# Attention softmax: one VectorE operation on two columns for a tile's threshold and the older tile's guarded sum

## The chip, the core and the metric

The kernel runs on one core of one Trainium2 chip. The core has a matrix engine (TensorE, PE in the profile, with its weight loads as PEld), a vector engine (VectorE, DVE), a scalar engine (ScalarE, ACT), GpSimd (POOL) and a queue that issues DMAs (SP). Each engine works through its own instruction queue in order; a wait at the head of a queue holds everything behind it. The metric is the device time of one execution in microseconds; the time of a kernel is the median of its runs.

## The reference

Attention over 2 batches, 8 heads, 576 rows and head dimension 64, then two mixture-of-experts layers on the 1152 rows of 512 columns. Only the attention is touched:

```python
def _attn_ref(q, k, v, tau):
    scores = scale * np.matmul(q, k.transpose(0, 1, 3, 2))
    thresh = np.max(scores, axis=-1, keepdims=True) - tau
    scores = np.where(scores >= thresh, scores, -1000000000.0)
    scores = scores - np.max(scores, axis=-1, keepdims=True)
    attn = np.exp(scores)
    attn = attn / (np.sum(attn, axis=-1, keepdims=True) + 1e-09)
    return np.matmul(attn, v)
```

Of each row the scores below the maximum minus tau are dropped, the rest goes through exp, and the row is divided by its sum plus 1e-9.

## The kernel before

The attention is cut into 72 units of 128 rows by 576 scores (`at.units`). They go through a software pipeline written out by hand: `step` runs once for each t, and in one step different units stand at different stages. Unit t+2 gets its scores on PE (`scores`), unit t+1 (called `a`) its row maximum and its exp (`top`, `line`, `exp`), unit t (called `d`) its mask with the row sum, its guarded sum, its reciprocal and its scaling (`mask`, `guard`, `norm`), unit t-2 (called `x`) is transposed on PE (`turn`) and split into a high and a low part (`hi` on ACT, `lo` on DVE), and units t-3 to t-5 are multiplied with V (`mix`, `out`). Nothing reorders this: the order of the calls in `step` is the order in each engine's queue.

On DVE one step is, for the two units together: the mask of `d` (L306, tile `ex`, which multiplies the exp by the comparison with the threshold and leaves the row sum in column 3 of `d`'s statistics tile `st`; reading the accumulator is a row of its own), the row maximum of `a` (L287, a reduction over 576 scores in PSUM), `guard` (L310, `d`'s sum plus 1e-9), `line` (L292, `a`'s threshold from its negated maximum and `on`, which holds tau), and the reciprocal of `d`'s guarded sum (L314). Behind these come `lo` (L341, L344, tiles `etl` and `eth`), `xf` (L388) and the low part of a hidden tile (L492, tile `hl`). The four units of the first head pair take their threshold with two operations (L294, L295) since their scores are not prescaled.

ACT reads column 0 of `a`'s statistics in its exp (L302; L300 in the first head pair). The mask waits for that exp. POOL scales `d`'s tile by the reciprocal (L316); PE transposes it two steps later (L324).

Into the free time of PE the steps put matrix products of the first two experts (`fill`, `expert_fill`: L483 and L511 on PE, L489 on ACT, L492 on DVE). What of these is left when the attention ends (at about 255 us) runs behind it, and the experts' layers follow to the end. All statistics of a unit lie in one `st` tile of 8 columns, of which 6 buffers rotate.

Of the kernel before, what the change touches and what calls it, by code (L numbers as in the profile page):

```python
# [9 lines left out]
F32 = mybir.dt.float32  # L10
F32R = mybir.dt.float32r
AF = mybir.ActivationFunctionType
ALU = mybir.AluOpType
# [6 lines left out]
P = 128  # L20
# [3 lines left out]
HS = S // 2  # L24
# [5 lines left out]
def attention_two_moe_kernel(ctx, tc, qP, kP, qT, kT, vp, tau, wg, w1, w1s, w2, w2s, dp, m2w1s, m2w2, m2w2s, out):  # L30
    nc = tc.nc
    V, A, G, T = nc.vector, nc.scalar, nc.gpsimd, nc.tensor
# [4 lines left out]
    def pool(stack, name, bufs=1, **kw):  # L37
        return stack.enter_context(tc.tile_pool(name=name, bufs=bufs, **kw))

    cp = pool(ctx, "const")  # L40
# [7 lines left out]
    ones = cp.tile([P, P], F32, name="ones")  # L48
# [5 lines left out]
    tau_sb = cp.tile([P, 1], F32, name="tau_sb")  # L54
    warm = cp.tile([P, 1], F32, name="warm")
    A.activation(warm, ones[:, 0:1], AF.Exp)
    esc = cp.tile([P, 1], F32, name="esc")
    lin = cp.tile([P, 2], F32, name="lin")
    on = cp.tile([P, 1], F32, name="on")
    wg_sb = cp.tile([P, KT, E1], F32, name="wg_sb")  # L60
    wg2 = cp.tile([P, KT, 2 * E1], F32R, name="wg2")
    dp_sb = cp.tile([P, NT, E2], F32, name="dp_sb")
# [7 lines left out]
    def gap(p, n):  # L70
        gaps.append(n)
        p.tile([P, n // 4], F32, name=f"gap{len(gaps)}")

    gap(cp, 224)
    xh = cp.tile([P, KT, N], F32R, name="xh")
    xl = cp.tile([P, KT, N], F32R, name="xl")

# [44 lines left out]
    class Attention:  # L122
# [159 lines left out]
                    T.matmul(sc[:m, hf, :HS], lhsT=q, rhs=kk[:, hf * HS:(hf + 1) * HS],  # L282
                             start=i == 0, stop=i == len(ops) - 1)

        def top(self, u):
            st = u["st"] = self.pl.tile([P, 8], F32, tag="st", name="st", bufs=6)
            V.tensor_reduce(st[:, 0:1], u["sc"][:, :, :HS], axis=AX.XY, op=ALU.max, negate=not u["q"][0][0]["ws"])  # L287

        def line(self, u):
            st = u["st"]  # L290
            if not u["q"][0][0]["ws"]:
                V.tensor_scalar(st[:, 2:3], st[:, 0:1], -1.0, on, op0=ALU.mult, op1=ALU.subtract)  # L292
                return
            V.tensor_scalar(st[:, 1:2], st[:, 0:1], lin[:, 0:1], None, op0=ALU.mult)  # L294
            V.tensor_scalar(st[:, 2:3], st[:, 0:1], lin[:, 1:2], None, op0=ALU.subtract)  # L295

        def exp(self, u):
            ex = u["ex"] = self.pl.tile([P, 2, HS], F32, tag="ex", name="ex", bufs=4)
            if u["q"][0][0]["ws"]:
                A.activation(ex, u["sc"][:, :, :HS], AF.Exp, bias=u["st"][:, 1:2], scale=esc)  # L300
            else:
                A.activation(ex, u["sc"][:, :, :HS], AF.Exp, bias=u["st"][:, 0:1])  # L302

        def mask(self, u):
            st, ex = u["st"], u["ex"]
            V.scalar_tensor_tensor(ex, u["sc"][:, :, :HS], st[:, 2:3], ex, op0=ALU.is_ge, op1=ALU.mult,  # L306
                                   accum_out=st[:, 3:4])

        def guard(self, u):
            V.tensor_scalar(u["st"][:, 4:5], u["st"][:, 3:4], 1e-9, None, op0=ALU.add)  # L310

        def norm(self, u):
            st = u["st"]
            V.reciprocal(st[:, 5:6], st[:, 4:5])  # L314
            exf = u["exf"] = u["ex"].rearrange("p a b -> p (a b)")
            G.tensor_scalar(exf, exf, st[:, 5:6], 1.0, op0=ALU.mult, op1=ALU.mult)  # L316

        def turn(self, u):
            eg, exf = u["eg"], u["exf"]
# [87 lines left out]
        def step(self, fill, side):  # L407

            us, t = self.units, self.t
            un = lambda i: us[i] if 0 <= i < len(us) else None  # L410
            self.load()
            nxt, a, d, x, c, z, y = (un(t + i) for i in (2, 1, 0, -2, -3, -4, -5))
            if x:
                self.turn(x)
            if d:
                self.mask(d)
            if a:
                self.top(a)
            if d:
                self.guard(d)  # L420
            if a:
                self.line(a)
            if d:
                self.norm(d)
            for part, u in ((2, y), (1, z), (0, c)):
                for g in u["mix"] if u else ():
                    if g["head"]["exact"]:
                        self.mix(g, part)
            if x:
                self.hi(x)  # L430
            for u, late in ((z, False), (y, True)):
                for g in u["mix"] if u else ():
                    if late == (g["head"]["exact"] and g["head"]["h"] < H - 1):
                        self.out(g)
            if a:
                self.exp(a)
            fill(0, bool(c and c["mix"]))
            if x:
                self.lo(x)
            if nxt:  # L440
                self.scores(nxt)
            self.run(self.later)
            for g in c["mix"] if c else ():
                if not g["head"]["exact"]:
                    self.mix(g, 0)
            fill(1, bool(c and c["mix"] or z and z["mix"]))
            self.run(self.late)
            for w in self.work.pop(t, ()):
                w()
            side()  # L450
            self.t += 1
            return self.t < len(us) + 5
# [85 lines left out]
    with ExitStack() as att:  # L538
        ap = pool(att, "attn", side="right")
        ps_s = pool(att, "ps_s", 2, space=PSUM)  # L540
        ps_t = pool(att, "ps_t", 1, space=PSUM)
        ps_r = pool(att, "ps_r", 1, space=PSUM)
        banks.pool = ps = pool(att, "ps_m", 2, space=PSUM)
        at = Attention(ap, ps_s, ps_t, ps_r, ps)
        for p in range(H // 2):
            at.add_pair(0, p, 0, 256, True, p == 0)
        nA0 = len(at.units)
        for p in range(H // 2):
            at.add_pair(0, p, 256, 320, False)
        nA1 = len(at.units)  # L550
        for p in range(H // 2):
            at.add_pair(1, p, 0, S, False)
        at.plan()
        room = [2 * FT]
        at.load()
        V.tensor_scalar(on, tau_sb, 0.0, None, op0=ALU.is_ge)
        V.tensor_scalar(esc, on, 0.125, None, op0=ALU.mult)
        V.tensor_scalar(lin[:, 0:1], on, -0.125, None, op0=ALU.mult)
        V.tensor_scalar(on, on, -BIG, BIG, op0=ALU.mult, op1=ALU.add)
        V.scalar_tensor_tensor(lin[:, 1:2], tau_sb, 8.0, on, op0=ALU.mult, op1=ALU.add)  # L560
        V.tensor_tensor(on, tau_sb, on, op=ALU.add)

        def side():
            if at.t >= -1:
                fetch(2)
            if at.t >= nA0 - 3 and raws and room[0] and (at.t % 3 < 2 if at.t < nA1 else room[0] > 2 or at.t % 2):
                room[0] -= 1
                cook()
            if at.t == 20:
                nc.sync.dma_start(wg_sb, wg)  # L570
                nc.sync.dma_start(dp_sb, dp)
            if at.t == 24:
                split(V, V, wg2[:, :, :E1], wg2[:, :, E1:], wg_sb)

        def free(n):
            room[0] += n

        X0, X1 = Expert(0), Expert(1)
        near, far = ((0, 0), (1, P)), ((2, 32), (3, 32 + P))
        todo = [(nA0 + 3, expert_fill(hp, X0, 0, 256, near, acc, None, 0, at.later, keep)),  # L580
                (nA1 + 3, expert_fill(hp, X0, 256, 320, far, acc, tail0[0], 0, at.later, free)),
                (nA1 + 3, expert_fill(hp, X1, 0, 256, near, y1, None, 0, at.later, keep)),
                (nA1 + 3, expert_fill(hp, X1, 256, 320, far, y1, tail0[1], 0, at.later, keep))]

        left, spent = [0], [0]

        def pull(n, end=True):

            for i in range(n):
                if not todo or at.t <= todo[0][0] or (left[0] == 1 and not end):  # L590
                    return i
                left[0] = next(todo[0][1], -1)
                if left[0] < 0:
                    todo.pop(0)
                if left[0] <= 0:
                    left[0] = 0
                    return i + 1
            return n

        def fill(phase, busy):  # L600
            if phase == 0:
                if 0 <= at.t < nA0 - 3 and at.t % 2 == 0:
                    room[0] -= 1
                    cook()
                spent[0] = pull(3)
            elif left[0] or not busy:
                pull(max((RA1 if at.t < nA1 + 3 else RA2) - spent[0], 0), True)

        while at.step(fill, side):
            pass  # L610
        at.flush()
        while left[0]:
            pull(1)
        at.flush()
        while raws:
            cook()
            fetch(2)
# [850 lines left out]
```

## Time and profile before

| what | value |
| --- | --- |
| time, median of 3 runs | 1312.94 us (1311.09 to 1314.7) |
| span of the profiled execution, first to last instruction | 1311.4 us |
| PE busy | 1276.5 us, 97% of the span |
| DVE busy | 888.6 us, 68% |
| ACT busy | 739.5 us, 56% |
| POOL busy | 901.8 us, 69% |
| instructions on DVE | 1879 |

The profiled execution has no time of its own beside its span; the span lies 1.5 us under the median of the three runs. A share of the span is an average over the attention, in which DVE, ACT and POOL work as densely as PE, and the expert layers, in which PE is nearly alone at its limit.

### The profile page before, as it was taken

The numbers are of one execution on the slowest core, as the hardware profiler recorded it, in microseconds if no ns is written. First come the engines' busy times: TensorE is split into PE (matmuls) and PEld (weight loads), VectorE is DVE, ScalarE is ACT, GpSimd is POOL, SyncE is SP. The second block draws the span as 40 slices with busy tenths as digits, with TensorE's granted clock in tenths as the row PEclk, the third lists the DMA queues.
The fourth block names the chain that finished last, engine by engine and source line by source line (L and its number), as shares of the span: only waits on it lengthen the run. The fifth ranks groups of instructions, "written<-read, shape, count | busy, mean of one in ns | idle before, by whom it ended". The sixth has DMA issues, their size and how long they took to land.

```text
span 1311.4 us, 25049 instructions
## 1 busy us (share of the span) xinstructions
PE 1276.5 (97%) x9373; PEld 1214.4 (93%) x9373; DVE 888.6 (68%) x1879; ACT 739.5 (56%) x1459; POOL 901.8 (69%) x988
## 2 busy tenths in 40 slices
PE   7998999999989999999999999999899999999998
PEld 4587988889879999999999999999889999999998
DVE  5799989447766666666666666667644666666667
ACT  6887877431445556555564655465545465555652
POOL 6886877432788576767777786768678567677760
PEclk9999999999999999999999999999999999999999
DMA  4542321110221111112111111111101111121102
GB/s 150 166 124 79 95 87 30 41 33 1 65 81 49 33 49 49 46 37 62 52 42 41 56 59 33 49 49 49 49 28 54 33 49 48 36 63 49 41 17 73
DMA packets 43226, 73.84 MB, mean 56 GB/s; under 512 B 5217, under 2 KB 12513, under 8 KB 43105
## 3 DMA queue, kind: packets, MB, share of 16 engines
q1 hardware_dynamic: 42816, 71.96, 18.7%
q8 instruction: 74, 1.21, 0.4%
q14 instruction: 48, 0.39, 0.1%
q10 hardware_dynamic: 288, 0.28, 0.1%
HBM read 69.86 MB, written 2.36 MB: 55 GB/s over the span
## 4 chain that ended last, share of the span: by engine, by line
PE 82%; DVE 8%; ACT 4%; POOL 3%; issue 2%; DMA 0%; DVEq 0%; POOLq 0%; ACTq 0%
PE mm L1044 33%; PE mm L1320 31%; PE mm L511 4%; PE mm L483 4%; PE sc L282 2%; PE mm L1150 2%; PE pv L359 2%; PE et L324 1%; DVE ex L306 1%; POOL wl L85 1%; DVE st L287 1%; DVE etl L341 1%; PE pv L368 1%; ACT ex L302 1%; PE pv L366 1%
## 5 line engine op out<-in xcount | busy, mean ns | idle before, releaser
L85 POOL TENSOR_TENSOR wl<-raw,wh 128x512 fp32r<-128x512 f32 x217 | 284.3, 1316 | 171.2 <-ACT wh L80 169.9
L1131 DVE SCALAR_TENSOR_TENSOR acc<-mm,p,acc 128x256 f32<-128x256 f32 (+1 forms) x428 | 195.5, 508 | 67.5 <-PE mm L1320 59.3
L1320 PE MATMUL mm<-wh,h 128*128 128x256 f32 x960 | 174.6, 281 | 0.0
L1051 ACT COPY snap<-mm 128x576 f32<-128x576 f32 x126 | 80.8, 642 | 149.7 <-DVE mm L1189 77.7
L80 ACT CAST wh<-raw 128x512 fp32r<-128x512 f32 x217 | 133.9, 627 | 46.5 <-PE mm L1320 26.4
L1044 PE MATMUL mm<-xh,wl 128*128 128x288 f32 x672 | 146.6, 299 | 4.3 <-DVE snap L1061 4.2
L1320 PEld LDWEIGHTS mm<-wh,h 128*128 128x128 f32 x960 | 147.5, 189 | 0.0
L1044 PE MATMUL mm<-xh,wh 128*128 128x288 f32 x672 | 143.9, 295 | 0.0
L1044 PE MATMUL mm<-xl,wh 128*128 128x288 f32 x672 | 143.5, 294 | 0.0
L1320 PE MATMUL mm<-wl,h 128*128 128x256 f32 x480 | 135.1, 282 | 3.2 <-ACT snap L1362 1.9
L1320 PE MATMUL mm<-wh,tails 128*128 128x256 f32 x696 | 126.7, 280 | 0.0
L85 POOL TENSOR_TENSOR wl<-sum,wh 128x512 fp32r<-128x512 f32 x82 | 107.4, 1309 | 10.8 <-ACT wh L80 10.8
L1044 PEld LDWEIGHTS mm<-xh,wl 128*128 128x128 f32 x672 | 106.8, 189 | 6.6 <-issue 3.2
L1044 PE MATMUL mm<-xth,wl 128*128 128x288 f32 x504 | 108.7, 297 | 4.2 <-ACT xth L80 1.9
L1044 PEld LDWEIGHTS mm<-xl,wh 128*128 128x128 f32 x672 | 108.2, 189 | 0.0
L1044 PEld LDWEIGHTS mm<-xh,wh 128*128 128x128 f32 x672 | 108.2, 189 | 0.0
L1044 PE MATMUL mm<-xtl,wh 128*128 128x288 f32 x504 | 107.8, 294 | 0.4 <-POOL xtl L85 0.4
L1044 PE MATMUL mm<-xth,wh 128*128 128x288 f32 x504 | 107.6, 295 | 0.0
L1320 PEld LDWEIGHTS mm<-wh,tails 128*128 128x128 f32 x696 | 106.6, 188 | 0.0
L80 ACT CAST wh<-sum 128x512 fp32r<-128x512 f32 x82 | 51.5, 628 | 82.2 <-POOL sum L770 68.7
L1320 PE MATMUL mm<-wl,tails 128*128 128x256 f32 x348 | 97.6, 280 | 0.0
L1320 PEld LDWEIGHTS mm<-wl,h 128*128 128x128 f32 x480 | 90.6, 189 | 3.9 <-ACT snap L1362 2.1
(235 smaller groups left out, 3508.4 us busy)
## 6 DMA issues: line engine op xcount, KB each, us to landing
raw<-in_w1s SPq DMA_DIRECT2D x56, 256.0 KB, 2.6
raw<-in_w2s SPq DMA_DIRECT2D x48, 256.0 KB, 2.6
raw<-in_w SPq DMA_DIRECT2D x40, 256.0 KB, 3.1
raw<-in_m2w1s SPq DMA_DIRECT2D x32, 256.0 KB, 2.6
raw<-in_m2w2s SPq DMA_DIRECT2D x28, 256.0 KB, 2.6
kr<-in_kT SPq DMA_DIRECT2D x22, 288.0 KB, 2.9
vr<-in_vp SPq DMA_DIRECT2D x24, 160.0 KB, 2.3
qr<-in_qT SPq DMA_DIRECT2D x8, 288.0 KB, 2.8
```

The costliest lines, as they stand in the source:

```text
L80: A.copy(hi, src)
L85: el.tensor_tensor(lo, src, f(hi), op=ALU.subtract)
L282: T.matmul(sc[:m, hf, :HS], lhsT=q, rhs=kk[:, hf * HS:(hf + 1) * HS], start=i == 0, stop=i == len(ops) - 1)
L287: V.tensor_reduce(st[:, 0:1], u["sc"][:, :, :HS], axis=AX.XY, op=ALU.max, negate=not u["q"][0][0]["ws"])
L359: T.matmul(pv[r0:r0 + D, :n], lhsT=hd["v"][:k, kt], rhs=self.e32[:k, kt, c], start=kt == 0, stop=kt == 4)
L483: T.matmul(ph[:, :n], lhsT=a[:, kt * P:(kt + 1) * P], rhs=x[:, kt, n0:n0 + n], start=i == 0 and kt == 0, stop=i == 2 and kt == KT - 1)
L511: T.matmul(py, lhsT=x, rhs=a, start=i == 0, stop=i == 3 * FT - 1)
L1044: T.matmul(ch[b][:, g, :HS], lhsT=w[:, (2 * g + kt) * P:(2 * g + kt + 1) * P], rhs=operand(u, kt, lo), start=first and j == 0, stop=j == l ...
L1051: A.copy(v[u], m)
L1131: V.scalar_tensor_tensor(a, src, s, a, op0=ALU.mult, op1=ALU.add)
L1150: T.matmul(py, lhsT=hid[x][:, kk, o:o + P], rhs=w[y], start=n == 0, stop=n == 3 * HF - 1)
L1320: T.matmul(m, lhsT=hid(x, kt + ko), rhs=wk[y], start=first and n == 0, stop=n == 5, skip_group_check=True)
```

## The change

The statistics of two units share one tile in each step. `step` takes a new tile `st`; the mask of `d` writes its sum into column 1 of it, the maximum of `a` goes to column 0 beside it, and one operation on two columns (SCALAR_TENSOR_TENSOR, times -1, minus the tile `floor`) makes columns 2 and 3: the threshold of `a` and minus the guarded sum of `d`. The reciprocal is then negative, and POOL's scaling multiplies by -1 instead of 1. `guard` is gone. `floor` is a new constant tile of two columns (tau or a very large negative number, and 1e-9); a gap in the constants shrinks by as much, so that the large tiles behind it stay where they were. In the first head pair the guard becomes a multiply and subtract of its own in `line`. In the very first step, which has no older unit, column 1 is filled with a copy of ones.

```diff
+    floor = cp.tile([P, 2], F32, name="floor")
-    gap(cp, 224)
+    gap(cp, 192)
...
-        def top(self, u):
-            st = u["st"] = self.pl.tile([P, 8], F32, tag="st", name="st", bufs=6)
+        def stats(self):
+            return self.pl.tile([P, 8], F32, tag="st", name="st", bufs=6)
+
+        def top(self, u, st):
+            u["st"] = st
             V.tensor_reduce(st[:, 0:1], u["sc"][:, :, :HS], axis=AX.XY, op=ALU.max, negate=not u["q"][0][0]["ws"])
-        def line(self, u):
-            st = u["st"]
-            if not u["q"][0][0]["ws"]:
-                V.tensor_scalar(st[:, 2:3], st[:, 0:1], -1.0, on, op0=ALU.mult, op1=ALU.subtract)
-                return
-            V.tensor_scalar(st[:, 1:2], st[:, 0:1], lin[:, 0:1], None, op0=ALU.mult)
-            V.tensor_scalar(st[:, 2:3], st[:, 0:1], lin[:, 1:2], None, op0=ALU.subtract)
+        def line(self, u, st):
+            if u is None:
+                V.tensor_scalar(st[:, 3:4], st[:, 1:2], -1.0, 1e-9, op0=ALU.mult, op1=ALU.subtract)
+            elif u["q"][0][0]["ws"]:
+                V.tensor_scalar(st[:, 3:4], st[:, 1:2], -1.0, 1e-9, op0=ALU.mult, op1=ALU.subtract)
+                V.tensor_scalar(st[:, 5:6], st[:, 0:1], lin[:, 0:1], None, op0=ALU.mult)
+                V.tensor_scalar(st[:, 2:3], st[:, 0:1], lin[:, 1:2], None, op0=ALU.subtract)
+            else:
+                V.scalar_tensor_tensor(st[:, 2:4], st[:, 0:2], -1.0, floor, op0=ALU.mult, op1=ALU.subtract)
...
-        def guard(self, u):
-            V.tensor_scalar(u["st"][:, 4:5], u["st"][:, 3:4], 1e-9, None, op0=ALU.add)
-            V.reciprocal(st[:, 5:6], st[:, 4:5])
+            V.reciprocal(st[:, 4:5], st[:, 3:4])
-            G.tensor_scalar(exf, exf, st[:, 5:6], 1.0, op0=ALU.mult, op1=ALU.mult)
+            G.tensor_scalar(exf, exf, st[:, 4:5], -1.0, op0=ALU.mult, op1=ALU.mult)
...
+            st = self.stats() if a or d else None
             if d:
-                self.mask(d)
+                self.mask(d, st)
+            elif a:
+                V.tensor_copy(st[:, 1:2], ones[:, 0:1])
             if a:
-                self.top(a)
-            if d:
-                self.guard(d)
-            if a:
-                self.line(a)
+                self.top(a, st)
+            if st is not None:
+                self.line(a, st)
             if d:
-                self.norm(d)
+                self.norm(d, st)
...
-        V.tensor_tensor(on, tau_sb, on, op=ALU.add)
+        V.tensor_tensor(floor[:, 0:1], tau_sb, on, op=ALU.add)
+        V.memset(floor[:, 1:2], 1e-9)
```

On DVE, two steps of the attention behind the first head pair, in the kernel before; behind each instruction stands the engine whose semaphore it waits for (`DVE_49` is DVE's own, `Activation_49` ACT's, `PE_49` PE's):

```order
L306 SCALAR_TENSOR_TENSOR ex,st<-sc,st,ex 128x576 [waits DVE_49,Activation_49]
L287 TENSOR_REDUCE st<-sc 128x1 [waits PE_49]
L310 TENSOR_SCALAR st<-st 128x1 [waits DVE_49]
L292 TENSOR_SCALAR st<-st,on 128x1 [waits DVE_49]
L314 RECIPROCAL st<-st 128x1 [waits DVE_49]
L377 TENSOR_TENSOR xl<-pv,xh 64x256 [waits Activation_49]
L306 SCALAR_TENSOR_TENSOR ex,st<-sc,st,ex 128x576 [waits DVE_49,Activation_49]
L287 TENSOR_REDUCE st<-sc 128x1 [waits PE_49]
L310 TENSOR_SCALAR st<-st 128x1 [waits DVE_49]
L292 TENSOR_SCALAR st<-st,on 128x1 [waits DVE_49]
L314 RECIPROCAL st<-st 128x1 [waits DVE_49]
```

The same two steps on DVE in the changed kernel, where the lines have moved (mask L313, maximum L291, the operation on two columns L302, reciprocal L317):

```order
L313 SCALAR_TENSOR_TENSOR ex,st<-sc,st,ex 128x576 [waits Activation_49]
L291 TENSOR_REDUCE st<-sc 128x1 [waits PE_49]
L302 SCALAR_TENSOR_TENSOR st<-st,floor 128x2 [waits DVE_49]
L317 RECIPROCAL st<-st 128x1 [waits DVE_49]
L380 TENSOR_TENSOR xl<-pv,xh 64x256 [waits Activation_49]
L313 SCALAR_TENSOR_TENSOR ex,st<-sc,st,ex 128x576 [waits Activation_49]
L291 TENSOR_REDUCE st<-sc 128x1 [waits PE_49]
L302 SCALAR_TENSOR_TENSOR st<-st,floor 128x2 [waits DVE_49]
L317 RECIPROCAL st<-st 128x1 [waits DVE_49]
```

L310 and L292 have become one instruction, and the mask has lost its wait for DVE's own semaphore. Before, L310 waits for the mask, L292 for the maximum and L314 for L310; now L302 waits for the maximum and L317 for L302.

The start of DVE's work in the kernel before, from the last constant (`on`) to the mask of the first unit:

```order
L561 TENSOR_TENSOR on<-tau_sb,on 128x1 [waits DVE_49]
L287 TENSOR_REDUCE st<-sc 128x1 [waits PE_49]
L294 TENSOR_SCALAR st<-st,lin 128x1 [waits DVE_49]
L295 TENSOR_SCALAR st<-st,lin 128x1
L306 SCALAR_TENSOR_TENSOR ex,st<-sc,st,ex 128x576 [waits DVE_49,Activation_49]
```

The same place in the changed kernel:

```order
L565 TENSOR_TENSOR floor<-tau_sb,on 128x1
L566 MEMSET floor 128x1
L422 COPY st<-ones 128x1
L291 TENSOR_REDUCE st<-sc 128x1 [waits PE_49]
L298 TENSOR_SCALAR st<-st 128x1 [waits DVE_49]
L299 TENSOR_SCALAR st<-st,lin 128x1 [waits DVE_49]
L300 TENSOR_SCALAR st<-st,lin 128x1
L313 SCALAR_TENSOR_TENSOR ex,st<-sc,st,ex 128x576 [waits DVE_49,Activation_49]
```

Three instructions have come in here: the constant 1e-9, the copy of ones ahead of the first maximum, and one operation between the maximum and L299. On DVE as a whole 68 steps lose one instruction and these three come in; no row of PE, ACT, POOL or SP has moved.

## Rows read from the trace of the kernel before

**Rows 1.** The page: busy time by engine, then the chain's shares.

```profile
PE 1276.5 (97%) x9373; PEld 1214.4 (93%) x9373; DVE 888.6 (68%) x1879; ACT 739.5 (56%) x1459; POOL 901.8 (69%) x988
...
PE 82%; DVE 8%; ACT 4%; POOL 3%; issue 2%; DMA 0%; DVEq 0%; POOLq 0%; ACTq 0%
```

**Rows 2.** Stretches (us): length, busy time of each engine, granted clock, DMA share.

```profile
60.00:80.00 20.00, 18.35 (x130) 15.76 (x131) 16.48 (x49) 15.81 (x33) 16.12 (x19) 1.00 0.45 128
...
120.00:140.00 20.00, 16.04 (x113) 14.86 (x114) 17.71 (x50) 14.32 (x27) 13.07 (x21) 1.00 0.25 69
...
180.00:200.00 20.00, 19.47 (x151) 18.09 (x150) 18.49 (x53) 17.75 (x37) 15.32 (x16) 1.00 0.34 98
...
260.00:280.00 20.00, 19.32 (x118) 15.98 (x117) 1.87 (x6) 4.41 (x14) 0.19 (x1) 0.91 0.00 1
```

**Rows 3.** Waits from 60 to 250 us: total, times, longest.

```profile
DVE etl L341 <- ACT eth L331: 13.4, 18, 1.5
...
PE et L324 <- DVE etl L341: 5.7, 9, 1.4
...
PE sc L282 <- DVE ex L306: 2.4, 4, 1.0
```

**Rows 4.** DVE in order of time, one step: start, duration, line.

```profile
189.26 0.76 DVE L287 TENSOR_REDUCE st<-sc 128x1 f32<-128x576 f32 x1
189.93 0.14 DVE L310 TENSOR_SCALAR st<-st 128x1 f32<-128x1 f32 x1
190.05 0.21 DVE L292 TENSOR_SCALAR st<-st,on 128x1 f32<-128x1 f32 x1
190.18 0.15 DVE L314 RECIPROCAL st<-st 128x1 f32<-128x1 f32 x1
190.25 0.67 DVE L341 TENSOR_TENSOR etl<-et,eth 128x512 fp32r<-128x512 f32 x1
```

**Rows 5.** DVE in order of time at the start.

```profile
4.69 0.16 DVE L560 SCALAR_TENSOR_TENSOR lin<-tau_sb,on 128x1 f32<-128x1 f32 x1
4.88 0.16 DVE L561 TENSOR_TENSOR on<-tau_sb,on 128x1 f32<-128x1 f32 x1
5.91 0.76 DVE L287 TENSOR_REDUCE st<-sc 128x1 f32<-128x576 f32 x1 [0.87 <-PE sc L273]
6.71 0.21 DVE L294 TENSOR_SCALAR st<-st,lin 128x1 f32<-128x1 f32 x1
```

**Rows 6.** DVE in order of time, the last unit: guard and reciprocal alone.

```profile
239.80 0.15 DVE L310 TENSOR_SCALAR st<-st 128x1 f32<-128x1 f32 x1
239.98 0.16 DVE L314 RECIPROCAL st<-st 128x1 f32<-128x1 f32 x1
```

**Rows 7.** Groups by form on DVE: count, busy us, mean ns, idle before.

```profile
L1107 DVE SCALAR_TENSOR_TENSOR taill<-mm,tailh 128x64 fp32r<-128x64 f32 x88 | 18.9, 215 | 0.0
```

**Rows 8.** The chain in order of time, its first and last passage: start, us, what.

```profile
17.74 0.06 DVE st L310
17.80 0.19 DVE st L292
17.99 0.08 DVE st L314
...
237.07 0.07 DVE st L314
```

**Rows 9.** DVE in order of time: idle behind the reciprocal, and its releaser.

```profile
191.16 0.42 DVE L492 SCALAR_TENSOR_TENSOR hl<-mm,hh 128x256 fp32r<-128x256 f32 x1 [0.24 <-ACT hh L489]
...
203.25 0.69 DVE L341 TENSOR_TENSOR etl<-et,eth 128x512 fp32r<-128x512 f32 x1 [0.23 <-ACT eth L331]
```

**Rows 10.** ACT in order of time: an exp that waited.

```profile
190.11 0.74 ACT L302 ACTIVATE ex<-sc,st 128x576 f32<-128x576 f32 x1 [0.49 <-DVE st L310]
```

**Rows 11.** Line 306: its wait instruction on DVE's queue, min/median/max ns.

```profile
L306 DVEq EVENT_SEMAPHORE  x68: 21/21/636, 7.1 to 238.5; - x68
```

More of the change, by code (lines that the diff above doesn't have):

```diff
@@ L299, in exp, with mask, norm @@
             if u["q"][0][0]["ws"]:
-                A.activation(ex, u["sc"][:, :, :HS], AF.Exp, bias=u["st"][:, 1:2], scale=esc)
+                A.activation(ex, u["sc"][:, :, :HS], AF.Exp, bias=u["st"][:, 5:6], scale=esc)
             else:
                 A.activation(ex, u["sc"][:, :, :HS], AF.Exp, bias=u["st"][:, 0:1])
[L304 to L307, printed above, removed]
-        def guard(self, u):
-            V.tensor_scalar(u["st"][:, 4:5], u["st"][:, 3:4], 1e-9, None, op0=ALU.add)
-        def norm(self, u):
-            st = u["st"]
-            V.reciprocal(st[:, 5:6], st[:, 4:5])
+        def mask(self, u, st):
+            ex = u["ex"]
+            V.scalar_tensor_tensor(ex, u["sc"][:, :, :HS], u["st"][:, 2:3], ex, op0=ALU.is_ge, op1=ALU.mult,
+                                   accum_out=st[:, 1:2])
+        def norm(self, u, st):
+            V.reciprocal(st[:, 4:5], st[:, 3:4])
             exf = u["exf"] = u["ex"].rearrange("p a b -> p (a b)")
-            G.tensor_scalar(exf, exf, st[:, 5:6], 1.0, op0=ALU.mult, op1=ALU.mult)
+            G.tensor_scalar(exf, exf, st[:, 4:5], -1.0, op0=ALU.mult, op1=ALU.mult)
         def turn(self, u):
```

## The prediction

> **What bounds the kernel now.** I read the page first, then the stretches, then the waits of the attention, then DVE in order of time, and last the chain in order of time. The page says that PE is busy for 97% of the span and DVE for 68%, and gives 82% of the chain that ended last to PE and 8% to DVE [rows 1]. That is an average over two very different parts. After the attention PE works 19.3 of 20 us while DVE works 1.9, as the stretch from 260 shows [rows 2]; nothing that this change touches is there. In the attention DVE works 16 to 18.5 of 20 us and PE 16 to 19.5 [rows 2], so the two share the bound, and a tenth of a microsecond on DVE can reach the end there. Whether it does is a question of who waits for whom: from 60 to 250 us PE waits 5.7 us in 9 places for DVE's `etl` and 2.4 us in 4 places for the mask [rows 3], and DVE itself waits 13.4 us in 18 places for ACT's `eth` [rows 3]. So in some steps DVE is ahead of its neighbours and in others behind; only in the latter does a change of its queue count. The change also keeps every row of PE, ACT, POOL and SP where it was, so whatever happens comes from DVE's few small operations and from what starts behind them.
>
> **What the step costs on DVE today.** In one step [rows 4] the maximum L287 starts at 189.26 and ends at 190.02; the guard L310 starts at 189.93, that is 0.67 after the maximum and before its end, since it needs only the older mask's sum; the threshold L292 starts at 190.05, 0.03 behind the maximum's end, since it needs that maximum; the reciprocal L314 starts 0.13 later at 190.18, and the next operation, `etl`, 0.07 later at 190.25. From the maximum's start to `etl` it is 0.99 us. What is to be seen here: the guard stands in the shadow of the maximum. It takes the time in which the threshold would be waiting anyway, and it is done (190.07) before the reciprocal can use it, with the threshold in between.
>
> **What the step costs after the change.** The guard goes and its column rides on the threshold. Gone with it is 0.12 us of DVE's queue (from 189.93 to 190.05), but in the shadow: the combined operation needs the maximum, so it can't start before 190.05 either. That an operation directly behind the maximum waits for its end is shown at the start, where none stands between: L287 starts at 5.91, L294 at 6.71, 0.80 later [rows 5]. Then comes the new part: the reciprocal needs the combined operation itself and stands directly behind it. The trace has two such pairs of a small operation and one that needs its result: 4.69 to 4.88, 0.19 us behind an operation of the same kind (SCALAR_TENSOR_TENSOR with one column, 0.16 us long) [rows 5], and 239.80 to 239.98, 0.18 us, a guard and its reciprocal with nothing between [rows 6]. Without the dependence it was 0.13. So the step becomes 0.80 + 0.19 + 0.07 = 1.06 us with the first pair and 0.79 + 0.18 + 0.07 = 1.04 with the second, against 0.99: **0.05 to 0.07 us more, I take 0.06**. One instruction less, and the step on DVE gets longer. The two-column form itself is not in the trace: its bounds are 0.16 us (one column [rows 5]) and 0.215 (64 columns of the same operation [rows 7]); two columns lie next to one, so 0.16. With the upper end the reciprocal would start 0.215 + 0.03 = 0.25 behind, and the step would grow by 0.13.
>
> **A rule that speaks the other way.** On this chain of tiny operations the trace shows 0.13 us from start to start without a dependence and 0.18 to 0.19 with one [rows 4 to 6]. The Trainium skill, page "VectorE: DVE Perf Modes", sections "The DRAIN you can't avoid" and "Rules for kernel authors", says that a semaphore between VectorE operations costs nothing extra and that one should minimize the count of operations, not of semaphores. By that rule the step would get shorter by one operation; this case's trace disagrees by the 0.05 us between its pairs, and I go by the trace.
>
> **The other edits.** The exp of the new tile (L302) needs only the maximum: in the step above it started at 190.11, 0.09 behind the maximum's end at 190.02 and before L292 was done at 190.26 [rows 4, 10], so the profile's naming of L310 as its releaser is only the nearest event. After the change it needs the same maximum: 0. POOL's scaling multiplies by -1 instead of 1 in the same instruction: 0; it starts 0.06 later with the reciprocal, and PE transposes that tile two steps later. If POOL had no such room, it would be the same 0.06 in that step. The mask loses its wait for DVE's own semaphore, in about 63 of 72 cases a separate wait instruction of 21 ns [rows 11]. If each lay on the path that would give back 63 x 0.02 = 1.3 us; I take 0, because it stands at the head of DVE's queue while the previous operation still runs or while the mask waits for the exp. The constant and the copy of ones come into the 0.87 us in which DVE waits for the first scores [rows 5]; without that cover they would be two small operations, 0.3 us once. The operation put in between the first maximum and L299 takes the place that the guard has in rows 4, in the maximum's shadow: 0.
>
> **How much of it reaches the end.** 68 steps get 0.06 us longer on DVE, 4.1 us together; the question is how many of them stand on the path. The chain in order of time goes through the reciprocal, that is through guard, threshold and reciprocal to the operation behind, 13 times: at 17.99 us first and at 237.07 last [rows 8]. In the other steps it leaves DVE at the maximum for ACT's exp, or is on PE. There the longer way has room: where the chain leaves for the exp, DVE often stands idle behind the reciprocal, 0.24 us until ACT's hidden tile or 0.23 us until ACT's `eth` [rows 9], four times the 0.06. So 13 x 0.06 = **0.8 us**. The span of the profiled execution would become 1311.4 + 0.8 = 1312.2 us; the median of the runs stands 1.5 us above the span, and I keep that: **1312.94 + 0.8 = 1313.7 us**, 0.06% more.
>
> **The rivals.**
> *The shorter queue wins.* If an operation that needs its neighbour's result follows as fast as any other, and the combined one follows the maximum as the guard does today (0.67), the step falls by the guard's 0.12 us. That is the skill's rule above as a mechanism of this kernel. On the 13 passages it gives 13 x 0.12 = 1.6 us, 1311.3; on all 68 steps it would be 8.2 us, 1304.8. Against it stand 5.91 to 6.71 and 239.80 to 239.98 [rows 5, 6], which show the waits themselves. Chance 0.09, of which 0.02 beyond 0.3%.
> *The delay goes through everywhere.* DVE's queue from mask to mask closes a circle (mask, maximum, threshold, reciprocal, `etl`, `xf`, `hl`, next mask). If it is the bound in nearly all steps, as the 18.5 of 20 us from 180 on would allow [rows 2], all 68 steps pay: 4.1 us, 1317.0. With the upper price of the two-column operation, 0.13 a step, it is 8.8 us, 1321.8. It decides from the point at which the 0.23 us of room [rows 9] are used up in most steps, and PE's own limit (19.5 of 20 us [rows 2]) speaks against it, since a late DVE is then met by a late PE. Chance 0.14, of which 0.05 beyond 0.3%.
> *Nothing arrives.* The 13 passages have parallel ways of nearly the same length through PE or ACT, and the delay is taken up by the next wait of DVE (18 for `eth` alone [rows 3]); or the mask's lost wait instruction pays for it: 1312.9, at the least 1312.94 - 1.3 = 1311.6. Chance 0.17.
>
> **How the numbers follow.** The forecast, 1313.7, has the other 0.60. The range takes in the forecast, the third rival with its bound, the first rival on the 13 passages (1311.3) and the second at the taken price (1317.0): **1311.3 to 1317.0**. Left out are the far ends of the first two rivals. A measurement of this kernel can tell about 0.3% (3.9 us) from no change; its three runs alone lie 3.6 us apart. Faster by more than that is only the first rival's far end, 0.02, and I put 0.03; slower by more is the second's upper part, 0.05; the rest, 0.92, is within.
>
> **What would show it.** In the changed trace the combined operation should start 0.79 to 0.80 us behind the maximum's start, last 0.16 us, and the reciprocal should start 0.18 to 0.19 behind it; from the maximum to the next ready operation 1.04 to 1.06 us where it was 0.99. If the reciprocal follows after 0.13 or the combined operation starts before the maximum's end, the dependence was priced wrongly and the first rival is right. DVE's instructions should fall by 65 and its busy time by some microseconds although the step gets longer, since overlapping operations count less and the gaps in front of the waits are no busy time: a reader who goes by the busy time would expect a gain. The attention's end (the last reciprocal, 239.98 us before) should come 0.5 to 1.5 us later; 4 us later is the second rival. The prediction is wrong if a stretch of the attention other than DVE's queue changes, for example if PE's waits for `etl` grow by more than a microsecond or PE's granted clock falls in a place where it did not before.

## The result, and the profile after

The changed kernel takes 1321.76 us (median of 4 runs, 1320.85 to 1322.96) against 1312.9 us before: 1.0070 times, with a 95% interval of 1.0059 to 1.0082, that is 8.9 us more. The forecast was 1313.7 us with a range up to 1317.0.

The profile's page (busy time by engine, then the chain's shares), the line groups by form on DVE (count, busy us, mean ns, idle before) and line 302 alone (min/median/max ns):

```profile
PE 1280.1 (97%) x9373; PEld 1215.5 (92%) x9373; DVE 908.3 (69%) x1814; ACT 740.5 (56%) x1459; POOL 902.0 (68%) x988
...
PE 78%; DVE 12%; ACT 4%; issue 3%; POOL 2%; DMA 0%; DVEq 0%; ACTq 0%; POOLq 0%
```

```profile
L302 DVE SCALAR_TENSOR_TENSOR st<-st,floor 128x2 f32<-128x2 f32 x68 | 34.0, 500 | 2.3
L317 DVE RECIPROCAL st<-st 128x1 f32<-128x1 f32 x72 | 11.8, 164 | 2.4
```

```profile
L302 DVE SCALAR_TENSOR_TENSOR st<-st,floor x68: 160/328/1411, 17.7 to 245.2; 128x2 f32<-128x2 f32 x68
```

DVE has 65 instructions fewer than before and is busy 19.7 us longer (888.6 us before [rows 1]). The whole of it, and more, is in one line: the operation on two columns lasts 0.16 us at its shortest, as forecast, and 1.41 us at its longest; its mean is 0.50. Nothing about two columns per row takes 1.4 us. A wide spread between the least and the most of one form is what the reader should stop at: the work is the same each time, so the rest is a wait, and it is counted as busy time, not as idle.

DVE in order of time (start, duration), one step where the operation is short and one where it is long:

```profile
188.13 0.74 DVE L291 TENSOR_REDUCE st<-sc 128x1 f32<-128x576 f32 x1
188.91 0.16 DVE L302 SCALAR_TENSOR_TENSOR st<-st,floor 128x2 f32<-128x2 f32 x1
189.11 0.16 DVE L317 RECIPROCAL st<-st 128x1 f32<-128x1 f32 x1
...
190.76 0.76 DVE L291 TENSOR_REDUCE st<-sc 128x1 f32<-128x576 f32 x1
191.55 1.41 DVE L302 SCALAR_TENSOR_TENSOR st<-st,floor 128x2 f32<-128x2 f32 x1
192.99 0.16 DVE L317 RECIPROCAL st<-st 128x1 f32<-128x1 f32 x1
```

POOL in order of time at the same place:

```profile
188.93 1.46 POOL L86 TENSOR_TENSOR kl<-kr,kh 128x576 fp32r<-128x576 f32 x1 [2.64 <-ACT kh L81]
190.37 0.74 POOL L319 TENSOR_SCALAR ex<-ex,st 128x576 f32<-128x576 f32 x1
191.50 1.44 POOL L253 TENSOR_TENSOR qs<-qr,qs 64x576 fp32r<-64x576 f32 x1 [0.39 <-ACT qs L252]
```

At 188.91 POOL was still idle (its next operation starts at 188.93) and the operation took 0.16 us. At 191.55 POOL's subtraction had started 0.05 us before; it ended at 192.94, and DVE's operation ended at 192.96. The two don't share a tile, and no semaphore stands between them. The same holds along the whole attention, step by step in the trace: L302 is longer than 0.2 us in 40 of 68 steps, and in 37 of these it ends 0.01 to 0.02 us behind the end of the POOL operation that was running when it started (two of the other three were released only by POOL's next operation, one ended 0.09 us behind). In the 28 steps in which it takes 0.16, POOL rested when it started, or had less than 0.15 us left. Together the 68 operations are 68 x (0.50 - 0.16) = 23 us longer than their work.

Where these microseconds go is seen in the stretches (busy times of the engines, then the granted clock) and in the waits from 60 to 250 us:

```profile
130.00:135.00 5.00, 4.61 (x25) 4.37 (x24) 3.03 (x9) 1.70 (x4) 1.49 (x2) 0.72 0.12 42
180.00:200.00 20.00, 18.53 (x130) 16.84 (x131) 18.85 (x42) 14.82 (x30) 14.98 (x17) 1.00 0.35 107
260.00:280.00 20.00, 19.32 (x107) 15.30 (x106) 1.70 (x4) 3.88 (x13) 5.44 (x15) 1.00 0.21 66
```

```profile
ACT ex L309 <- DVE st L291: 14.5, 17, 1.5
PE et L327 <- DVE etl L344: 9.6, 16, 1.4
```

```profile
L317 DVE RECIPROCAL st<-st x72: 152/164/167, 9.6 to 248.3; 128x1 f32<-128x1 f32 x72
```

From 180 to 200 us PE did 130 matmuls, where it did 151 before [rows 2]. Its waits for `etl` grew from 5.7 us in 9 places [rows 3] to 9.6 us in 16. The last reciprocal, 239.98 before [rows 6], comes at 248.3: 8.3 of the 23 us arrive at the end of the attention and are carried to the end of the kernel. Set side by side with the kernel before, reciprocal by reciprocal, none in the first 60 us comes more than 0.4 us later; the lateness builds between about 85 and 225 us. TensorE's clock moved too. From 130 to 135 us, after PE had been busy for only 2.69 of the 5 us before, the granted clock was 0.72, part of the stretch at its lower level of 1.2 GHz and part at 2.4; in the kernel before it was 1.00 in that stretch. Across this place the reciprocals' lateness grew from 2.9 to 4.8 us. The other way round, from 20 to 25 us the clock was 0.76 in the kernel before and 1.00 in the changed one, so what the first 60 us show is not free of the clock either. The loss doesn't hang on the fall at 130 us: the first experiment below has the same wait and a clock of 1.00 there, and its last reciprocal comes at 248.3 as well.

### The profile page after: what moved, and what is told of

It reads as the page before. It is cut to its first block, busy times and chain, and to the rows that moved or that the text cites. A ratio compares the mean times of both kernels' runs of the same rounds, so it can differ in the third digit from the quotient of the medians.

```text
span 1321.2 us, 24921 instructions
## 1 busy us (share of the span) xinstructions
PE 1280.1 (97%) x9373; PEld 1215.5 (92%) x9373; DVE 908.3 (69%) x1814; ACT 740.5 (56%) x1459; POOL 902.0 (68%) x988
## 4 chain that ended last, share of the span: by engine, by line
PE 78%; DVE 12%; ACT 4%; issue 3%; POOL 2%; DMA 0%; DVEq 0%; ACTq 0%; POOLq 0%
PE mm L1049 33%; PE mm L1325 31%; PE mm L487 3%; PE mm L1155 3%; PE mm L515 3%; DVE ex L313 2%; DVE st L291 2%; PE sc L283 1%; DVE etl L344 1%; DVE st L302 1%; PE et L327 1%; ACT ex L309 1%; DVE acc L1136 1%; PE pv L371 1%; PE pv L362 1%
```

## The experiments

Theory A: DVE's operation waits because of what it reads. Two streams out of SBUF on DVE can't run beside a POOL operation on SBUF, so it waits for POOL's running operation. Rival B: the longer dependent chain (maximum, operation, reciprocal) costs the time. Rival C: any operation over two columns in SBUF waits, also with one tensor. Each kernel's operation is shown by its line (count: min/median/max ns).

**One number instead of the second tensor.**

```diff
-                V.scalar_tensor_tensor(st[:, 2:4], st[:, 0:2], -1.0, floor, op0=ALU.mult, op1=ALU.subtract)
+                V.tensor_scalar(st[:, 2:4], st[:, 0:2], -1.0, floor[:, 0:1], op0=ALU.mult, op1=ALU.subtract)
```

> The changed kernel with one operand changed: the operation on two columns subtracts one number per row (tau, column 0 of floor, as a scalar operand) from both columns instead of the two-column tile floor, so that it reads one tensor from SBUF and not two. The guard is then tau instead of 1e-9. Order, count and waits stay those of the changed kernel. Theory A (the operation waits for a running POOL operation because it reads two tensors from SBUF): it lasts about 0.2 us in all 68 steps, not 0.16 to 1.41 with a mean of 0.50, and the kernel takes about 1313 to 1315 us. Rival B (the longer dependent chain, maximum to operation to reciprocal, costs the time, and the long operation only shows a late neighbour): it stays near 1321.8 us. Rival C (any operation on two SBUF columns takes the shared way into SBUF, with one tensor too): its duration still follows POOL's, mean near 0.5, and the time stays near 1321.8.

Measured: 1324.87 us, 1.0088 times before (1.0072 to 1.0103).

```profile
L302 DVE TENSOR_SCALAR st<-st,floor x68: 228/398/1507, 18.0 to 245.3; 128x2 f32<-128x2 f32 x68
```

Theory A as I had put it missed: with one tensor the operation waits as before, 0.23 to 1.51 us, and the time is no better. In the kernel before, the same TENSOR_SCALAR with a scalar per row on one column (L292) lasted this in its 68 steps, in 43 of which a POOL operation ran from its start to its end:

```profile
L292 DVE TENSOR_SCALAR st<-st,on x68: 212/214/217, 17.8 to 236.9; 128x1 f32<-128x1 f32 x68
```

So rival C holds for this form: one column never waits, two columns do. A remains open for the form with two tensors.

**The kernel before, with the second tensor alone.**

```diff
-                V.tensor_scalar(st[:, 2:3], st[:, 0:1], -1.0, on, op0=ALU.mult, op1=ALU.subtract)
+                V.scalar_tensor_tensor(st[:, 2:3], st[:, 0:1], -1.0, on, op0=ALU.mult, op1=ALU.subtract)
```

> The kernel before with one operand changed: the threshold (L292, one column) takes tau from the tile on as a second tensor (SCALAR_TENSOR_TENSOR) instead of as a scalar per row. The result is the same, the guard stays in the maximum's shadow, no instruction is gone or moved. Theory A: L292 lasts until POOL's running operation ends, mean 0.4 to 0.5 us instead of 0.21, up to about 1.4, and the kernel is slower by 6 to 10 us, 1319 to 1323. Rival B (dependent chain): no change, 1313, since the chain is that of before. Rival C: no change, since it is one column.

Measured: 1319.26 us, 1.0045 times before (1.0028 to 1.0062), 6.2 us more. The last reciprocal comes at 244.2.

```profile
L292 DVE SCALAR_TENSOR_TENSOR st<-st,on x68: 159/322/1400, 18.1 to 241.1; 128x1 f32<-128x1 f32 x68
```

One column, the guard still there, the reciprocal not dependent on it: only the operand, and with it the instruction's form, differs, and the wait is there with the same spread. B and C both said no change. So there are two ways into the same wait: two tensors in SBUF (one column is enough), or one tensor with two columns in this form.

**The dependent chain alone.**

```diff
-                V.scalar_tensor_tensor(st[:, 2:4], st[:, 0:2], -1.0, floor, op0=ALU.mult, op1=ALU.subtract)
+                V.tensor_scalar(st[:, 2:3], st[:, 0:1], -1.0, 0.02, op0=ALU.mult, op1=ALU.subtract)
...
-            V.reciprocal(st[:, 4:5], st[:, 3:4])
+            k = 2 if self.t >= 3 and self.t + 1 < len(self.units) else 3
+            V.reciprocal(st[:, 4:5], st[:, k:k + 1])
```

> The changed kernel with the operation on two columns replaced by one on the threshold's column alone, with constants only (times -1, minus 0.02), and the reciprocal taken of that threshold, so that it still has to wait for the operation directly before it. The tiles are then scaled by another number than the row sum. This is the dependent chain that the prediction priced, without a second tensor. Theory A: from the maximum's start to the reciprocal 0.79 + 0.18, to the next operation 1.04 us, and the kernel at 1313 to 1315 us (0.8 us over before was forecast for this chain). Rival B: near 1321.8 us, since the chain is the same as in the changed kernel.

Measured: 1314.36 us, 1.0009 times before (1.0000 to 1.0018), 1.3 us more by the medians. DVE in order of time:

```profile
189.36 0.76 DVE L291 TENSOR_REDUCE st<-sc 128x1 f32<-128x576 f32 x1
190.15 0.15 DVE L302 TENSOR_SCALAR st<-st 128x1 f32<-128x1 f32 x1
190.34 0.17 DVE L318 RECIPROCAL st<-st 128x1 f32<-128x1 f32 x1
190.42 0.67 DVE L345 TENSOR_TENSOR etl<-et,eth 128x512 fp32r<-128x512 f32 x1
```

From the maximum to `etl` it is 1.06 us, the step that the prediction worked out. By the times the chain costs 1.3 us, by the interval 0 to 2.4; in the profile the last reciprocal comes at 240.22, only 0.24 us later than before. So the 0.8 us of the prediction is neither refuted nor confirmed. Rival B falls: the chain without the operand costs about a seventh of the loss.

**Shorter POOL operations.**

```diff
-            G.tensor_tensor(lo, raw, f(hi), op=ALU.subtract)
+            for c in (slice(0, DM // 2), slice(DM // 2, DM)):
+                G.tensor_tensor(lo[:, c], raw[:, c], f(hi)[:, c], op=ALU.subtract)
...
+                A.copy(hd["kh"], hd["k"])
+                for c in (slice(0, HS), slice(HS, S)):
+                    G.tensor_tensor(hd["kl"][:, c], hd["k"][:, c], f(hd["kh"][:, c]), op=ALU.subtract)
```

(and the subtraction for `qs` in the same way)

> The changed kernel with three of POOL's long subtractions in the attention (the low parts of the weights, of K and of Q, 1.3 to 1.45 us each) cut into two halves by columns, about 0.75 to 0.8 us each; the result is the same, POOL gets about 76 more instructions and some 0.15 us more for each. DVE's instructions stay. Theory A: the operation on two columns waits at most for one half: its longest falls from 1.41 to about 1.0 (0.85 for a half or an uncut operation of that length and 0.16), its mean from 0.50 to about 0.35, and the kernel gains 2 to 5 us on the changed one, 1317 to 1320. Rival B, or a general slowing by shared memory bandwidth: the mean stays at 0.5 and the time at 1321 to 1323, since POOL has more to do and no less data to move.

Measured: 1318.33 us, 1.0047 times before (1.0031 to 1.0064), 3.4 us less than the changed kernel, although POOL does more.

```profile
L306 DVE SCALAR_TENSOR_TENSOR st<-st,floor x68: 160/302/1819, 17.9 to 243.3; 128x2 f32<-128x2 f32 x68
```

The mean fell from 0.50 to 0.40 (0.35 was expected), and in 11 of its 44 longer cases the operation is released between the two halves. But the longest grew to 1.82, where about 1.0 was expected; POOL in order of time at that place, where DVE's operation started at 169.89 and ended at 171.71:

```profile
169.42 0.75 POOL L323 TENSOR_SCALAR ex<-ex,st 128x576 f32<-128x576 f32 x1
170.13 0.74 POOL L86 TENSOR_TENSOR xl<-xf,xh 128x256 fp32r<-128x256 f32 x1
170.82 0.87 POOL L86 TENSOR_TENSOR vhl<-vr,vhl 128x320 fp32r<-128x320 f32 x1
```

It sat through the ends of two POOL operations and was released by the third. A change of POOL's operations alone, with DVE's left as they were, moves DVE's durations: that is what A and C say, and B can't.

**The whole change, with `floor` in PSUM.** The first form:

```diff
-            sc = u["sc"] = self.ps_s.tile([P, 2, 512], F32, tag="sc", name="sc")
+            sc = u["sc"] = self.scs[self.units.index(u) % 2]
...
-                V.scalar_tensor_tensor(st[:, 2:4], st[:, 0:2], -1.0, floor, op0=ALU.mult, op1=ALU.subtract)
+                V.scalar_tensor_tensor(st[:, 2:4], st[:, 0:2], -1.0, u["sc"][:, 0, HS:HS + 2], op0=ALU.mult, op1=ALU.subtract)
...
+        for sc in at.scs:
+            V.tensor_copy(sc[:, 0, HS:HS + 2], floor)
```

> The changed kernel whole, with one operand in another memory: the two-column tile floor lies in PSUM, in two columns of each scores buffer that the scores don't use, written once at the start (two copies more on DVE, and the two scores buffers are taken in turn by hand). The operation on two columns then reads one tensor from SBUF and one from PSUM; the result is the same. Theory A (two streams from SBUF on DVE wait for a running POOL operation): the operation lasts 0.16 to 0.25 us in all 68 steps, the last reciprocal comes near 240 to 241 us, not 248.3, and the time is that of the chain without tensor, 1313.5 to 1315. If the operation waits for POOL for any reason other than what it reads from SBUF (its place in the queue, its two columns, its writes), it stays at a mean of 0.5 us and the time at 1320 to 1323.

Measured: 1317.88 us, 1.0037 times before (1.0025 to 1.0049).

```profile
L303 DVE SCALAR_TENSOR_TENSOR st<-st,sc x68: 156/157/159, 19.5 to 240.4; 128x2 f32<-128x2 f32 x68
```

The wait is gone in all 68 steps (in 45 of them a POOL operation ran throughout): the same operation, columns, place, chain and POOL, another memory for one operand. It also bounds rival C: here two columns are read from SBUF and nothing waits, so two columns alone are not enough in every form. The time is above what was expected, though. The first reciprocal comes 1.8 us late, because the copies into the scores' banks hold up the first matmuls (they start at 5.39 us, behind the copies, where they started at 3.53). So the copies were moved:

```diff
-        for sc in at.scs:
-            V.tensor_copy(sc[:, 0, HS:HS + 2], floor)
...
+            if t in (0, 1):
+                V.tensor_copy(self.scs[t][:, 0, HS:HS + 2], floor)
             if d:
                 self.mask(d, st)
```

> The kernel with floor in PSUM again, but the two copies into the scores buffers come in the first two steps, directly ahead of the mask, where DVE waits for the exp, and no longer ahead of the first scores (which they delayed by 1.8 us). Everything else as there: the whole change, with one tensor from SBUF and one from PSUM. If the rest of that kernel's 5 us over before was this start, the time is 1314 to 1316 and the last reciprocal comes at 240.5 to 242 us; the remainder over 1312.9 is the price of the dependent chain (1.06 against 0.99 us a step, 1.3 us measured without a second tensor). If it stays at 1317 to 1318, something else in the change costs 4 us beside the wait for POOL.

Measured: 1317.28 us, 1.0031 times before (1.0016 to 1.0046), with runs from 1313.15 to 1318.92. The operation again lasts 0.16 us in all steps, and the last reciprocal comes at 242.3, 2.3 us after that of before. So the expected 1314 to 1316 was missed by about 1.3 us, and the other branch was met: something else costs some 4 us. The trace shows a cost that this experiment itself brought in, in both of its forms: ACT's exp, which reads the same scores buffer, now starts behind the threshold operation and no longer behind the maximum. DVE, then ACT, in order of time in this kernel:

```profile
190.78 0.75 DVE L292 TENSOR_REDUCE st<-sc 128x1 f32<-128x576 f32 x1
191.57 0.16 DVE L303 SCALAR_TENSOR_TENSOR st<-st,sc 128x2 f32<-128x2 f32 x1
...
191.82 0.74 ACT L310 ACTIVATE ex<-sc,st 128x576 f32<-128x576 f32 x1 [0.69 <-DVE st L303]
```

The exp starts 0.29 us behind the maximum's end. It is at least 0.28 in 67 of 68 steps (once 0.23), where in the kernel before, the changed kernel and the chain alone it was 0.09 at the least. ACT waited for the operation in 20 places; 20 x 0.19 = 3.8 us is an estimate, from these rows, of the most that this can cost. How much of it arrives no run shows, nor why the exp waits.

The clock differs as well. Between 120 and 135 us the lateness grows by 1.7 us; the granted clock there falls to 0.73, as the mean of a stretch of 5 us, after a pause of PE for `etl` (1.38 us), while in the kernel before such a pause (1.35 us) is followed by a clock of 1.00. From 20 to 25 us it is the kernel before whose clock is lower (0.76), and at 30 us this one is 1.1 us ahead. The stretch of this kernel:

```profile
125.00:130.00 5.00, 4.04 (x22) 3.81 (x21) 4.67 (x13) 1.69 (x3) 1.70 (x3) 0.73 0.29 92
```

This is read from one profile of each kernel. So the two runs with `floor` in PSUM show what the operation waits for, but their times are no clean price of the wait.

**One operation less in the maximum's shadow.**

```diff
-            V.reciprocal(st[:, 5:6], st[:, 4:5])
+            V.reciprocal(st[:, 5:6], st[:, 3:4])
...
             if d:
-                self.guard(d)
+                self.norm(d)
             if a:
                 self.line(a)
-            if d:
-                self.norm(d)
```

> The kernel before without the guard (1e-9 is left out; every row sum is at least about 1, so that the sum rounds to the same number), the reciprocal put in the guard's place, in the maximum's shadow, and the threshold behind it. This takes one operation away from the same place as the change does, but with one column each, no second tensor, and the dependent operation still in the maximum's shadow. From the maximum's start: reciprocal 0.67, threshold 0.79, next operation 0.92, where it was 0.99. With 13 passages of the chain, 13 x 0.07 = 0.9 us less: 1312.1, within what can be told from no change; if all 68 steps passed it on, 4.8 us less, 1308.2. The step's saving is the reverse of the dependent chain's loss (1.06 against 0.99, which cost 1.3 us), so about 1 us of gain is expected.

Measured: 1312.38 us, 0.9994 times before (0.9985 to 1.0002): not to be told from no change. The step is the 0.92 us that was worked out, and the last reciprocal comes 0.5 us earlier, at 239.44. None of the kernels is measurably better than the kernel before; this one is the only one whose interval reaches below 1.

## Why the prediction was wrong

The step that failed is the price of the two-column operation: "The two-column form itself is not in the trace: its bounds are 0.16 us (one column [rows 5]) and 0.215 (64 columns of the same operation [rows 7])". Both rows are of the right operation and of the wrong situation. The one at 4.69 us reads two tensors from SBUF, but stands where POOL does nothing. L1107 runs beside POOL, but one of its tensors lies in PSUM. I bounded the price by the number of columns, and in this form columns weren't what it hangs on (two tensors waited with one column too). The two-column operation measured 0.50 us on average and 1.41 at its longest, because it waits for POOL's running operation.

The trace of before had rows with both conditions. One is L1107 itself: four of its operations read `snap` from SBUF in the place of `mm`. They took 0.21 us twice, where POOL rested, and 0.41 and 0.76 beside POOL (min/median/max):

```profile
L1107 DVE SCALAR_TENSOR_TENSOR taill<-snap,tailh x4: 213/314/760, 343.5 to 976.4; 128x64 fp32r<-128x64 f32 x4
```

The other is a small subtraction on DVE (32 columns) with both tensors in SBUF, beside a POOL operation. DVE in order of time:

```profile
83.47 0.18 DVE L82 CAST wg<-wg_sb 128x32 fp32r<-128x32 f32 x1
83.68 0.92 DVE L85 TENSOR_TENSOR wg<-wg_sb,wg 128x32 fp32r<-128x32 f32 x1
```

And POOL:

```profile
83.68 0.88 POOL L85 TENSOR_TENSOR xl<-xf,xh 128x320 fp32r<-128x320 f32 x1 [0.43 <-ACT xh L80]
84.52 0.88 POOL L85 TENSOR_TENSOR vhl<-vr,vhl 128x320 fp32r<-128x320 f32 x1
```

0.92 us for 32 columns, ending with POOL's operation. (In the changed kernel the same two operations start together at 84.13 us, and DVE's takes 0.20.) With these rows the upper bound would have been the length of a POOL operation, up to 1.45 us, and the case "the operation waits for POOL" would have been a rival of its own: POOL was busy for 13 to 16 of 20 us in the attention [rows 2].

The Trainium skill has the rule, on the page "SBUF — State Buffer", section "Who interferes with whom": a VectorE instruction with two SBUF inputs (beside a GpSimd instruction that reads SBUF), or in one of the modes that use both ports, contends for a port pair that it shares with GpSimd, and whoever comes second waits for the whole instruction of the other; one with at most one SBUF input outside these modes does not. The runs here agree: two tensors 0.16 to 1.82 us, one tensor with two columns 0.23 to 1.51, one column and one tensor 0.21 to 0.22, one tensor in SBUF and one in PSUM 0.16 throughout. That TENSOR_SCALAR on two columns ran in such a mode would fit; no run shows the mode itself. It was the rule that spoke against this change, and the prediction weighed another.

The other steps, in their order:

- **What bounds the kernel: right.** A loss on DVE in the attention does reach the end. Behind the attention little changed: PE is busy 19.3 of 20 us from 260 us in both, and from the last reciprocal to the end of the span it is 1071.4 us before and 1072.9 after; the runs of the experiments lie between 1069.9 and 1073.2.
- **The step today and its shadow: right.** Without the wait the new step measured 1.06 us, against 1.04 to 1.06 worked out and 0.99 before.
- **The rule on semaphores: right to set aside.** A dependent pair took 0.19 us from start to start (190.15 to 190.34), against 0.13 without a dependence.
- **The other edits at nothing: not contradicted.** The exp still starts as early as 0.09 us behind the maximum, and the first reciprocal comes no later than before (9.62 against 9.67 us), so the operations at the start were hidden. The mask's lost wait was not tried alone.
- **13 passages, 0.8 us: within the measurement for the 0.06 us that it was made for**, with 1.3 us by the times (interval 0 to 2.4) and 0.24 at the last reciprocal. For the 23 us of waiting it was never meant: 8.3 us came through, about a third, and more of the chain lies on DVE (12% of the span, 8% before).
- **The second rival** names 1321.8 us at its far end, the time that was measured. It is a coincidence: it needed 0.13 us in each of 68 steps, all on the path; what happened is 0.34 us on average, in bursts of up to 1.25, a third of it on the path. Its chance beyond 0.3% was put at 0.05 because its price was capped at 0.215.
- **The signs:** the combined operation started 0.78 to 0.79 us behind the maximum, as listed, and the reciprocal 0.04 behind its end; that it should "last 0.16 us" failed. DVE's busy time rose by 19.7 us where it should have fallen, and the attention's end came 8.3 us later where 0.5 to 1.5 was expected. Both examples that the prediction named as signs of its being wrong came true: PE's waits for `etl` grew by 3.9 us, and PE's granted clock fell where it did not before.

How the loss of 8.9 us divides: the dependent chain alone cost 1.3 us (interval 0 to 2.4). The changed kernel lies 7.4 us above that one by the times and about 8 by the ratios (1.0070 against 1.0009); that is the wait, with whatever the clock did behind it. In the kernel before, the wait alone cost 6.2 us (3.7 to 8.1). Moving `floor` to PSUM gave back 4.5 to 5.1 us, less than the whole, and there the exp came later too. What stays open is the clock's part, and how the 2 to 6 us by which the last kernel with `floor` in PSUM lies above before divide between the chain, the late exp and the clock; its runs spread over 5.8 us.

## What to carry to other kernels

Price a small VectorE operation by what it reads before counting its columns: with two tensors from SBUF beside a busy GpSimd it lasts until GpSimd's operation ends, and the profile books the wait as busy time. One tensor is no safe price either: in one form the second column brought the same wait. When looking for bounding rows, match the memory of each operand and the neighbour engine's load, and read min, median and max of a form, not its mean. An operation that stands in the shadow of a wait is nearly free (taking the guard out moved the attention's end by 0.5 us): merging it into the one behind the wait saves next to nothing and adds a dependence. When an operand is moved to another memory to test a cause, look at who else reads that buffer: here the exp came 0.19 us later.

## What the runs showed of the hardware

- TENSOR_SCALAR with a scalar per row, one tensor in SBUF: 0.21 to 0.22 us in 68 of 68 cases with one column, 0.23 to 1.51 with two columns. I had not expected one more column to bring the wait.
- Putting one of two SBUF operands into PSUM took the wait away entirely (0.156 to 0.159 us in 68 of 68).
- A waiting DVE operation is mostly released at the end of the POOL operation that runs; once it waited through the ends of two and was released by the third (1.82 us). In the changed kernel it was 37 of 40.
- A pause of PE of nearly the same length in the same place (1.35 and 1.38 us) was followed by a granted clock of 1.00 in one kernel and of 0.73, as the mean of 5 us, in another. With PE busy for 2.66 of 5 us the clock stayed at 1.00 in the next 5 us in one kernel (the first with `floor` in PSUM), and with 2.69 it was 0.72 in another (the changed one).
